# Routed experts: input sums and one pair sum on VectorE, second weight matrix issued by ScalarE

## The chip, the cores and the metric

The kernel runs on one core of a Trainium2 chip (trn2). The metric is the device time of one execution in microseconds (us). One core has a matmul engine (TensorE, PE in the profile), three engines for elementwise work (VectorE or DVE, ScalarE or ACT, GpSimd or POOL) and SyncE (SP), which issues DMAs here. Each engine works through its own queue in order, and an instruction that waits holds all that stands behind it in that queue.

## The reference

Three layers follow one another on 4608 tokens of width 512, all float32: attention in chunks of 64 tokens, a dense two-matrix layer with a squared ReLU, and a routed layer in which each token goes to the one of 8 experts with the largest logit.

```python
attn = softmax(scale * q_c @ k_c^T); x = attn @ v_c      # 8 heads, 9 chunks of 64, 8 batches
h = np.maximum(x @ w_in, 0.0); x = h * h @ w_out          # 512 -> 2048 -> 512
logits = x @ w_gate + modality_bias[modality_id]
e_idx = np.argmax(logits, axis=1)
for e in range(E):                                        # E = 8, F = 1024
    h = np.maximum(x[mask] @ w1[e], 0.0)
    out[mask] = gate_w[mask, None] * (h @ w2[e])
```

With these inputs two experts get all the tokens, 2325 and 2283. In blocks of 256 tokens that makes 10 and 9 blocks, 19 in all.

## The kernel before

Every float32 value that a matmul reads is held as two float16 words, a high word (the rounded value, made on ScalarE) and a low word (the rest, a subtraction on VectorE or GpSimd). A product is then three matmuls of word pairs. The kernel runs in two stages: attention and the dense layer on 36 tiles of 128 tokens, and then the routed layer on pairs, blocks of 256 tokens that share an expert. The tokens of a pair are gathered from DRAM by GpSimd DMAs (`x_gather`), transposed by SyncE DMAs (`x_tr`), and their outputs scattered by GpSimd DMAs (`put`), two of each for one pair.

The routed layer multiplies 2x2 block matrices with seven block products in place of eight, so a pair has seven products of the first matrix (`pair_mm1`, n = 0 to 6) and seven of the second (`pair_mm2`), and sums around them:

- `x_sum0` makes two 128x512 sums of high and low words of the input (lines 968, 969) and four 128x256 sums and differences (lines 971 to 974). `x_sum1` splits these into high words on ScalarE and low words on GpSimd (line 983).
- `pair_c` takes a product of the first matrix out of PSUM as soon as it is there and builds the four hidden blocks c11, c12, c21, c22.
- `pair_s` makes the sums of hidden blocks that the second matrix needs and splits them, in seven steps. Step 1 has the pair sum c21 = c11 - c21 on GpSimd (line 1073). Steps 5 and 6 split c12 and c21 with the low word on GpSimd (`split_h`, line 1065).
- `pair_o` takes the output products out of PSUM, scaled by the token's gate, on ScalarE (tile ms) and VectorE (tile raw), and calls `put`.

The order is written out by hand. A slot is one product with what is emitted beside it. After the first seven slots a slot of the second matrix of pair p (`run2`) alternates with a slot of the first matrix of pair p + 2 (`run1`). `plan_side(p)` is called in the slot s in which pair p's seventh product of the first matrix is emitted, and puts steps of `pair_s`, `x_sum0`, `x_sum1` and the gathers into slots s + k:

```python
if p > 2:
    once(x_tr, p + 2)
    later(3, x_gather, p + 3)
if p > 1:
    later(8 if p > 2 else 10, x_sum0, p + 2)
    later(11 if p > 2 else 13, x_sum1, p + 2)
```

The seven steps of `pair_s` have k = 1 to 7 there for pairs 2 to 17, and k = 1, 1, 2, 2, 3, 3, 4 for pair 18. For p in the middle, output products of pair p - 1 (fourth to seventh) stand at odd k up to 7, those of pair p from k = 9 on, and first-matrix products of pair p + 1 at even k. The seventh output product of pair p - 1 goes into the PSUM bank that the second one of pair p takes over, at s + 11; the two operations that empty it are on VectorE in `pair_o`. The third output product goes to the bank that the profile calls xq. The first half of a pair's output is put after its fifth product and the second half after its seventh; a put waits for the put before it to have landed.

The main part has 19 pairs (0 to 18, NP = 18). Further pairs stand in `tail`, under a condition that these inputs don't meet. `later` lets gathers and input steps through only up to pair 18; `once(x_tr, p + 2)` is not limited that way, so the transposes of pairs 19 and 20 are issued too.

The weights of a pair's expert stand in two large SBUF tiles (big0 for the first matrix, big1 for the second), which hold the dense layer's weights before. They were split earlier and wait in DRAM (wsp). Loading one matrix takes four DMAs of 0.5, 1, 1 and 1 MB (`load_part`, line 902; blocks 0, 1 to 2, 3 to 4, 5 to 6 of the seven). `early_w` loads the first expert's, all on SyncE: the first matrix before the dense layer ends; of the second matrix part 0 in the second slot of pair 1, part 1 behind the last dense tile's transposes and ahead of pair 2's, parts 2 and 3 in the sixth and seventh slot of pair 1. `late_w` issues the loads of later pairs under a condition, met where the expert changes. `x2_evac`, `x2_tr` and `route_a` to `route_c` are the evacuation, transposes and routing of a dense tile; the last tile's result is needed by the map of the later pairs (`map_b1` to `map_b3`, whose transposes on TensorE write the tile tp).

Of the kernel before, what the change touches and what calls it, by code (L numbers as in the profile page):

```python
# [31 lines left out]
def kernel(  # L32
# [13 lines left out]
    nc = tc.nc  # L46
# [850 lines left out]
        spread_pairs(ti, fs, EARLY, LATE)  # L897

    WB = [bigs[x][:, 0:14336].rearrange("p (b l k n) -> p b l k n", b=7, l=2, k=2 + 2 * x) for x in range(2)]
    def load_part(x, e, k, **kw):  # L900
        a, b = (2048 * n for n in GROUPS[k])
        nc.sync.dma_start(out=bigs[x][:, a:b], in_=wsp[bass.ds(e, 1), x, :, a:b].rearrange("a p c -> (a p) c"), **kw)

    def early_w(x, k):
        assert stored[0] >= 7 * READY * (x + 1), (x, k, stored)
        if k == 0:
            mp["ew"] = nc.sync.value_load(mp["rga"][0:1, 0:1], min_val=0, max_val=E - 1)
        load_part(x, mp["ew"], k)

    def late_w(x, p, n):  # L910
        if p >= PAIRS or n not in [b - 1 for _, b in GROUPS] or (x, p, n) in gone:
# [41 lines left out]
        x_sum1(p)  # L953

    def x_sum0(p):
        eng = nc.gpsimd
        _, t, sh, sl = xbuf(p)
        if p < 2:
            f = [a2_p.tile([128, 512], F32, tag="ee", name="xf") for _ in range(2)]
            s = [a2_p.tile([128, 2, 256], F32, tag="pt", name="xs32") for _ in range(2)]  # L960
            sv = [s[j // 2][:, j % 2] for j in range(4)]
        else:
            o = 12288
            f = [bigs[2][:, o + h * 1024:o + h * 1024 + 1024].bitcast(F32) for h in range(2)]
            s = [bigs[2][:, o + 2048 + h * 1024:o + 3072 + h * 1024].bitcast(F32).rearrange("p (j c) -> p j c", j=2) for h in range(2)]
            sv = [s[j // 2][:, j % 2] for j in range(4)]
        for h in range(2):
            (eng if p < 2 else nc.vector).tensor_tensor(out=f[h].rearrange("p (k n) -> p k n", k=4), in0=t[:, h, 0:4],
                                                        in1=t[:, h, 4:8], op=ALU.add)
        q = [[f[h][:, j * 256:j * 256 + 256] for j in range(2)] for h in range(2)]  # L970
        eng.tensor_tensor(out=sv[0], in0=q[1][0], in1=q[1][1], op=ALU.add)  # L971
        eng.tensor_tensor(out=sv[1], in0=sv[0], in1=q[0][0], op=ALU.subtract)  # L972
        eng.tensor_tensor(out=sv[2], in0=q[0][0], in1=q[1][0], op=ALU.subtract)
        eng.tensor_tensor(out=sv[3], in0=q[0][1], in1=sv[1], op=ALU.subtract)  # L974
        mp["xs", p] = s
# [91 lines left out]
    def pair_s(p, n):  # L1067
        c11, c12, c21, c22 = cbuf(p)
        if n == 0:
            split_h(p, 5, c22, AF.Relu)  # L1070
        elif n == 1:
            stt(c22, c22, 0.0, c21, ALU.max, ALU.add)
            nc.gpsimd.tensor_tensor(out=c21, in0=c11, in1=c21, op=ALU.subtract)
        elif n == 2:
            split_h(p, 1, c22)
        elif n == 3:
            nc.vector.tensor_tensor(out=c11, in0=c11, in1=c22, op=ALU.subtract)
            stt(c12, c12, 0.0, c11, ALU.max, ALU.add)
        elif n == 4:
            split_h(p, 3, c11, scale=-1.0)  # L1080
        elif n == 5:
            split_h(p, 4, c12, eng=nc.gpsimd)
        else:
            split_h(p, 6, c21, eng=nc.gpsimd)

    def pair_mm2(p, n):
        blk_, bank, first = PRODUCTS[n]
# [270 lines left out]
    for su, (b0, nt, sb) in enumerate(supers):  # L1358
# [8 lines left out]
        for t, qq in M2 if su == 0 else [(t, qq) for t in range(nt) for qq in range(4)]:  # L1367
# [17 lines left out]
            if i == NTILE - 1:  # L1385
                ch += [(T + 16.0, map_b1, ()), (T + 18.0, map_b1b, ()), (T + 21.0, map_b2, ()), (T + 22.0, meta_gather, (LATE, "b")), (T + 29.0, meta_turn, (LATE, "b")), (T + 31.0, map_b3, ())]
                ch += [(T + 34.0 + p, once, (x_gather, 4 + p)) for p in range(2)]
                ch[2:2] = [(T + d[0] + 0.1, early_w, (1, 1))]
            at_chain(ch)
        if su == len(supers) - 1:  # L1390
            at_time(TM1 + 8.0, map_a1c)
            at_time(TM1 - 8.0, rest, "a", [quad(b)[:, 0:512] for b in range(4)])
            for k in range(4):
                at_time(TM1 + 0.1 + 2.65 * k, early_w, 0, k)
            at_time(T + 0.1, early_w, 1, 0)
            for n in range(7):
                at_time(T - STEP + 1.33 * n, pair_s, 0, n)
    TEND = T
# [14 lines left out]
    with tc.manual_schedule():  # L1413
# [50 lines left out]
        def later(k, fn, *a):  # L1464
            if fn not in (x_gather, x_tr, x_sum0, x_sum1):
                side.setdefault(len(slots) + k, []).append((fn, a))
            elif a[0] <= NP:
                side.setdefault(len(slots) + k, []).append((once, (fn, *a)))

        def plan_side(p):  # L1470
            for n, k in enumerate((1, 1, 2, 2, 3, 3, 4) if p == NP else (1, 2, 3, 4, 5, 6, 7) if p > 1 else (1, 3, 4, 6, 8, 9, 10)):
                later(k, pair_s, p, n)
            if p > 2:
                once(x_tr, p + 2)
                later(3, x_gather, p + 3)
            if p > 1:
                later(8 if p > 2 else 10, x_sum0, p + 2)
                later(11 if p > 2 else 13, x_sum1, p + 2)

        slots = []  # L1480
# [4 lines left out]
        for k, fn, q in ((4, x_tr, 2), (6, x_tr, 3), (8, x_sum0, 2), (10, x_sum1, 2), (14, x_sum0, 3), (17, x_sum1, 3), (27, x_tr, 4)):  # L1485
            later(k, fn, q)
        for n in range(7):
            if n > 4:
                early_w(1, n - 3)
            run1(1, n)  # L1490
        for k in range(7 * (NP + 1)):
            run2(k // 7, k % 7)
# [85 lines left out]
```

## Time and profile before

| | |
|---|---|
| three runs | 1266.19, 1273.77, 1274.33 us, median 1273.77 |
| profiled execution | 1271.61 us, its span 1269.9 us |
| mean granted TensorE clock | 0.982 |
| TensorE matmuls | 1196.7 us busy, 94% |
| VectorE | 837.7 us, 66% |
| ScalarE | 709.3 us, 56% |
| GpSimd | 678.3 us, 53% |
| DMA | 166.26 MB, mean 131 GB/s |

The span is the time from the first to the last instruction. Busy times are those of instructions in progress, and engines overlap. A row of the timeline has the start in the span, the duration (for merged instructions that of the group, with xN), the engine, the line of the kernel, the operation, and the tiles that it writes and reads with their shape. What stands in brackets is the engine's idle time just before, and what ended it. SPq rows are DMA issues of SyncE, which are not counted as busy.

### The profile page before, as it was taken

Reading aid. Unit: us, or ns where it says so; the run is one execution under the profiler, and the core shown is the slowest. Engines: PE = TensorE matmul, PEld = TensorE weight load, DVE = VectorE, ACT = ScalarE, POOL = GpSimd, SP = SyncE. Lnnn points to the kernel's source line nnn. Section 1 sums busy time; section 2 is a strip of 40 time slices with the busy share of each in tenths; the row PEclk is TensorE's granted clock in tenths of the full one; section 3 lists DMA queues with packets and bytes.
Section 4 is the critical chain, followed back from the end, with each engine's and each line's share of the span. In section 5 each row is a group of like instructions: output and inputs, shape, how many; then the busy total and the mean of one; then the engine's idle time right before and its main releaser. Section 6 shows DMA issues by size and latency. Waiting matters only on the chain. (4 is left out here: it accounts for less than half of the span.)

```text
span 1269.9 us, 30528 instructions
## 1 busy us (share of the span) xinstructions
PE 1196.7 (94%) x12046; PEld 746.0 (59%) x12046; DVE 837.7 (66%) x1750; ACT 709.3 (56%) x1284; POOL 678.3 (53%) x626
## 2 busy tenths in 40 slices
PE   5898999999999999999999999999799998999993
PEld 4444444444445444445444444457699997889992
DVE  6899665685775765776856654625676776667751
ACT  6887673673763853854854744524355554555551
POOL 4487353471571652634651653653677766667642
PEclk9899999999999999999999999999899999999997
DMA  9456426656447356465555333257343356633431
GB/s 374 159 171 162 112 34 183 162 155 167 141 133 194 85 142 174 125 182 129 131 151 149 101 87 96 79 156 138 100 109 76 85 119 185 156 73 84 79 61 36
DMA packets 167701, 166.26 MB, mean 131 GB/s; under 512 B 124218, under 2 KB 124254, under 8 KB 166002
## 3 DMA queue, kind: packets, MB, share of 16 engines
q1 hardware_dynamic: 160226, 144.64, 42.9%
q0 software_dynamic: 7312, 19.50, 5.0%
q8 instruction: 96, 1.57, 0.6%
q14 instruction: 67, 0.55, 0.2%
HBM read 211.40 MB, written 49.16 MB: 205 GB/s over the span
## 5 line engine op out<-in xcount | busy, mean ns | idle before, releaser
L627 PE MATMUL hp<-xtall,big 128*128 128x512 f16 x1728 | 386.6, 381 | 2.6 <-ACT r L92 2.6
L642 PE MATMUL op<-big,big 128*128 128x512 f16 x1728 | 386.4, 381 | 0.5 <-POOL big L607 0.5
L642 PEld LDWEIGHTS <-big 128*128 128x128 f16 x1728 | 165.3, 98 | 194.6 <-issue 4.4
L607 POOL TENSOR_TENSOR big<-g,big 128x512 f16<-128x512 f32 x144 | 175.4, 1223 | 193.1 <-DVE g L95 92.1
L627 PEld LDWEIGHTS <-big 128*128 128x128 f16 x1728 | 164.2, 98 | 192.9 <-issue 6.4
L1024 PEld LDWEIGHTS <-big 128*128 128x128 f16 x3192 | 191.0, 99 | 6.6 <-issue 2.5
L1024 PE MATMUL hq<-big,big 128*128 128x128 f16 x2040 | 129.0, 220 | 0.7 <-DVE raw L1054 0.7
L288 POOL TENSOR_TENSOR raw<-raw 128x512 f32<-128x512 f32 x64 | 92.4, 1468 | 57.0 <-DVE ms L95 32.2
L92 ACT ACTIVATE r<-hp 128x512 f32<-128x512 f32 x138 | 81.4, 590 | 61.4 <-PE hp L627 43.9
L92 ACT ACTIVATE big<-r,bls 128x512 f16<-128x512 f32 x138 | 98.4, 714 | 3.0 <-DVE bls L101 0.6
L1092 PEld LDWEIGHTS <-xtall 128*128 128x128 f16 x840 | 80.4, 99 | 24.6 <-issue 10.8
L1092 PE MATMUL oq<-big,xtall 128*128 128x256 f16 x600 | 74.9, 276 | 14.4 <-DMA big<-wsp 7.1
L95 DVE SCALAR_TENSOR_TENSOR g<-r,bq 128x512 f32<-128x512 f32 x74 | 72.3, 979 | 20.3 <-ACT r L92 18.2
L1092 PEld LDWEIGHTS <-ho 128*128 128x128 f16 x756 | 71.9, 98 | 16.6 <-issue 9.2
L487 POOL TENSOR_TENSOR ps<-ee,ps 128x512 f16<-128x512 f32 x32 | 41.6, 1301 | 69.7 <-ACT ps L92 55.4
L712 POOL DMA_INDIRECT meta<-mt,di x36 | 39.1, 1086 | 72.2 <-issue 35.0
L1092 PE MATMUL oq<-big,ho 128*128 128x256 f16 x540 | 66.2, 273 | 8.2 <-DVE raw L95 6.0
L92 ACT ACTIVATE xs<-op 128x512 bf16<-128x512 f32 x36 | 21.4, 593 | 91.8 <-PE op L642 84.3
L92 ACT ACTIVATE xtall<-cq 128x512 f16<-128x512 f32 x70 | 43.8, 626 | 43.0 <-DVE cq L1048 14.5
L92 ACT ACTIVATE g<-r,bls 128x512 f32<-128x512 f32 x64 | 46.2, 722 | 27.4 <-POOL big L607 22.7
L92 ACT ACTIVATE big<-big 128x512 f16<-128x512 f32 (+1 forms) x58 | 37.1, 649 | 43.7 <-POOL big L972 23.1
L92 ACT ACTIVATE ho<-raw 128x512 f16<-128x512 f32 x63 | 39.4, 625 | 39.5 <-DVE raw L1048 15.6
(293 smaller groups left out, 1897.2 us busy)
## 6 DMA issues: line engine op xcount, KB each, us to landing
big<-wsp SPq DMA_DIRECT2D x114, 1024.0 KB
big<-wsp SPq DMA_DIRECT2D x38, 512.0 KB
wsp<-ms SPq DMA_DIRECT2D x75, 256.0 KB
qk<-in_qk_dram SPq DMA_DIRECT2D x36, 512.0 KB
raw<-in_w_dram SPq DMA_DIRECT2D x32, 512.0 KB
wsp<-wss SPq DMA_DIRECT2D x37, 256.0 KB
vv<-in_v_dram SPq DMA_DIRECT2D x36, 256.0 KB
x2d<-xs SPq DMA_DIRECT2D x36, 256.0 KB
```

What stands on the lines that cost most here:

```text
L92: nc.scalar.activation(out=out, in_=in_, func=func, **kw)
L95: nc.vector.scalar_tensor_tensor(out=out, in0=in0, scalar=s, in1=in1, op0=op0, op1=op1, **kw)
L288: nc.gpsimd.tensor_tensor(out=o, in0=i0, in1=i1, op=op)
L487: nc.gpsimd.tensor_tensor(out=a["ps"][:, 1], in0=pf, in1=a["ps"][:, 0], op=ALU.subtract)
L607: nc.gpsimd.tensor_tensor(out=lo, in0=q32.rearrange("p (f n) -> p f n", f=nf), in1=hi, op=ALU.subtract)
L627: nc.tensor.matmul(hp[:, q_ * n:(q_ + 1) * n], lhsT=wi[:, la, kk, f * 128:f * 128 + 128], rhs=x[:, lb, kk, :], start=i == 0, stop=i == 3 * ...
L642: nc.tensor.matmul(ps, lhsT=g[:, la, f, t * 128:t * 128 + 128], rhs=wo[:, lb, f, :], start=f == 0 and n == 0, stop=f == KF - 1 and n == 2)
L712: nc.gpsimd.indirect_dma_start(out=meta[:, :], out_offset=bass.IndirectOffsetOnAxis(ap=di[:, 0:1].bitcast(U32), axis=0), in_=mt, in_offset ...
L1024: nc.tensor.matmul(ps[:, f * 128:f * 128 + 128], lhsT=WB[0][:, n, la, kk, f * 128:f * 128 + 128], rhs=xa(lb, kk), start=first and f + m + ...
L1092: nc.tensor.matmul(ps, lhsT=hb[:, la, f * 128:f * 128 + 128], rhs=WB[1][:, n, lb, f, :], start=first and f + m == 0, stop=True, skip_group ...
```

## The change

- In `x_sum0` the four 128x256 sums of pairs 2 and later go from GpSimd to VectorE, where their two 128x512 sums are already; for pairs 0 and 1 all six stay on GpSimd.
- In `pair_s` the pair sum of step 1 goes from GpSimd to VectorE.
- Steps 5 and 6 of `pair_s` keep their low word on GpSimd, except in the last pair (18), where it goes to VectorE. For pairs 2 to 17 they move from slots s + 6 and s + 7 to s + 13 and s + 14.
- `x_sum0` moves from slot s + 8 to s + 9 for pairs above 4.
- The first expert's second matrix is issued by ScalarE in place of SyncE, with its own register load of the expert's number. Parts 0 and 1 stand ahead of the last dense tile's evacuation, parts 2 and 3 behind it.
- The gathers of pairs 19 and 20 are let through in the main part.

```diff
--- before.py
+++ after.py
@@ -897,15 +897,16 @@
         spread_pairs(ti, fs, EARLY, LATE)
 
     WB = [bigs[x][:, 0:14336].rearrange("p (b l k n) -> p b l k n", b=7, l=2, k=2 + 2 * x) for x in range(2)]
-    def load_part(x, e, k, **kw):
+    def load_part(x, e, k, eng=None, **kw):
         a, b = (2048 * n for n in GROUPS[k])
-        nc.sync.dma_start(out=bigs[x][:, a:b], in_=wsp[bass.ds(e, 1), x, :, a:b].rearrange("a p c -> (a p) c"), **kw)
+        (eng or nc.sync).dma_start(out=bigs[x][:, a:b], in_=wsp[bass.ds(e, 1), x, :, a:b].rearrange("a p c -> (a p) c"), **kw)
 
     def early_w(x, k):
         assert stored[0] >= 7 * READY * (x + 1), (x, k, stored)
+        eng = (nc.sync, nc.scalar)[x]
         if k == 0:
-            mp["ew"] = nc.sync.value_load(mp["rga"][0:1, 0:1], min_val=0, max_val=E - 1)
-        load_part(x, mp["ew"], k)
+            mp["ew", x] = eng.value_load(mp["rga"][0:1, 0:1], min_val=0, max_val=E - 1)
+        load_part(x, mp["ew", x], k, eng)
 
     def late_w(x, p, n):
         if p >= PAIRS or n not in [b - 1 for _, b in GROUPS] or (x, p, n) in gone:
@@ -953,7 +954,7 @@
         x_sum1(p)
 
     def x_sum0(p):
-        eng = nc.gpsimd
+        eng = nc.gpsimd if p < 2 else nc.vector
         _, t, sh, sl = xbuf(p)
         if p < 2:
             f = [a2_p.tile([128, 512], F32, tag="ee", name="xf") for _ in range(2)]
@@ -965,7 +966,7 @@
             s = [bigs[2][:, o + 2048 + h * 1024:o + 3072 + h * 1024].bitcast(F32).rearrange("p (j c) -> p j c", j=2) for h in range(2)]
             sv = [s[j // 2][:, j % 2] for j in range(4)]
         for h in range(2):
-            (eng if p < 2 else nc.vector).tensor_tensor(out=f[h].rearrange("p (k n) -> p k n", k=4), in0=t[:, h, 0:4],
+            eng.tensor_tensor(out=f[h].rearrange("p (k n) -> p k n", k=4), in0=t[:, h, 0:4],
                                                         in1=t[:, h, 4:8], op=ALU.add)
         q = [[f[h][:, j * 256:j * 256 + 256] for j in range(2)] for h in range(2)]
         eng.tensor_tensor(out=sv[0], in0=q[1][0], in1=q[1][1], op=ALU.add)
@@ -1070,7 +1071,7 @@
             split_h(p, 5, c22, AF.Relu)
         elif n == 1:
             stt(c22, c22, 0.0, c21, ALU.max, ALU.add)
-            nc.gpsimd.tensor_tensor(out=c21, in0=c11, in1=c21, op=ALU.subtract)
+            nc.vector.tensor_tensor(out=c21, in0=c11, in1=c21, op=ALU.subtract)
         elif n == 2:
             split_h(p, 1, c22)
         elif n == 3:
@@ -1079,9 +1080,9 @@
         elif n == 4:
             split_h(p, 3, c11, scale=-1.0)
         elif n == 5:
-            split_h(p, 4, c12, eng=nc.gpsimd)
+            split_h(p, 4, c12, eng=nc.vector if p == NP else nc.gpsimd)
         else:
-            split_h(p, 6, c21, eng=nc.gpsimd)
+            split_h(p, 6, c21, eng=nc.vector if p == NP else nc.gpsimd)
 
     def pair_mm2(p, n):
         blk_, bank, first = PRODUCTS[n]
@@ -1385,14 +1386,14 @@
             if i == NTILE - 1:
                 ch += [(T + 16.0, map_b1, ()), (T + 18.0, map_b1b, ()), (T + 21.0, map_b2, ()), (T + 22.0, meta_gather, (LATE, "b")), (T + 29.0, meta_turn, (LATE, "b")), (T + 31.0, map_b3, ())]
                 ch += [(T + 34.0 + p, once, (x_gather, 4 + p)) for p in range(2)]
-                ch[2:2] = [(T + d[0] + 0.1, early_w, (1, 1))]
+                ch[1:1] = [(T + 0.1 * k, early_w, (1, k)) for k in range(2, 4)]
+                ch[0:0] = [(T, early_w, (1, k)) for k in range(2)]
             at_chain(ch)
         if su == len(supers) - 1:
             at_time(TM1 + 8.0, map_a1c)
             at_time(TM1 - 8.0, rest, "a", [quad(b)[:, 0:512] for b in range(4)])
             for k in range(4):
                 at_time(TM1 + 0.1 + 2.65 * k, early_w, 0, k)
-            at_time(T + 0.1, early_w, 1, 0)
             for n in range(7):
                 at_time(T - STEP + 1.33 * n, pair_s, 0, n)
     TEND = T
@@ -1464,17 +1465,17 @@
         def later(k, fn, *a):
             if fn not in (x_gather, x_tr, x_sum0, x_sum1):
                 side.setdefault(len(slots) + k, []).append((fn, a))
-            elif a[0] <= NP:
+            elif a[0] <= NP or fn is x_gather and a[0] <= NP + 2:
                 side.setdefault(len(slots) + k, []).append((once, (fn, *a)))
 
         def plan_side(p):
-            for n, k in enumerate((1, 1, 2, 2, 3, 3, 4) if p == NP else (1, 2, 3, 4, 5, 6, 7) if p > 1 else (1, 3, 4, 6, 8, 9, 10)):
+            for n, k in enumerate((1, 1, 2, 2, 3, 3, 4) if p == NP else (1, 2, 3, 4, 5, 13, 14) if p > 1 else (1, 3, 4, 6, 8, 9, 10)):
                 later(k, pair_s, p, n)
             if p > 2:
                 once(x_tr, p + 2)
                 later(3, x_gather, p + 3)
             if p > 1:
-                later(8 if p > 2 else 10, x_sum0, p + 2)
+                later(9 if p > 2 else 10, x_sum0, p + 2)
                 later(11 if p > 2 else 13, x_sum1, p + 2)
 
         slots = []
@@ -1485,8 +1486,6 @@
         for k, fn, q in ((4, x_tr, 2), (6, x_tr, 3), (8, x_sum0, 2), (10, x_sum1, 2), (14, x_sum0, 3), (17, x_sum1, 3), (27, x_tr, 4)):
             later(k, fn, q)
         for n in range(7):
-            if n > 4:
-                early_w(1, n - 3)
             run1(1, n)
         for k in range(7 * (NP + 1)):
             run2(k // 7, k % 7)
```

## Rows read from the trace of the kernel before

**Rows 1.** Page of the profile, its first part, whole span.

```profile
PE 1196.7 (94%) x12046; PEld 746.0 (59%) x12046; DVE 837.7 (66%) x1750; ACT 709.3 (56%) x1284; POOL 678.3 (53%) x626
```

**Rows 2.** Timeline, TensorE: start us, duration us, engine, line, operation, out<-in.

```profile
935.61 1.47 PE L1092 MATMUL xq<-big,xtall 128*128 128x256 f16 x12
...
1032.45 1.47 PE L1092 MATMUL xq<-big,ho 128*128 128x256 f16 x12
...
1212.94 1.47 PE L1092 MATMUL xq<-big,xtall 128*128 128x256 f16 x12
...
1231.49 1.47 PE L1092 MATMUL xq<-big,ho 128*128 128x256 f16 x12
```

**Rows 3.** Waits of TensorE, 905 to 1245 us: total us, times, longest.

```profile
PE oq L1092 <- DVE raw L95: 11.6, 13, 2.1
...
PE oq L1092 <- ACT ms L92: 1.7, 2, 1.0
PE tp L759 <- DVE mgc L751: 1.2, 1, 1.2
PE hq L1024 <- DVE raw L1054: 0.7, 2, 0.3
```

**Rows 4.** Timeline of one pair, all engines; idle before in brackets.

```profile
986.77 3.06 DVE L95 SCALAR_TENSOR_TENSOR xtall<-cq,xtall 128x512 f16<-128x512 f32 x1 [0.70 <-ACT xtall L92]
986.97 2.30 POOL L1065 TENSOR_TENSOR ho<-raw,ho 128x512 f16<-128x512 f32 x2
...
989.75 0.86 DVE L95 SCALAR_TENSOR_TENSOR raw<-oq,fsb,ms 128x256 f32<-128x256 f32 x2
...
990.67 1.47 PE L1092 MATMUL oq<-big,ho 128*128 128x256 f16 x12 [0.59 <-DVE raw L95]
...
994.77 0.72 POOL L974 TENSOR_TENSOR big<-big 128x256 f32<-128x256 f32 x1
994.83 0.48 DVE L95 SCALAR_TENSOR_TENSOR raw<-xq,fsb,ms 128x256 f32<-128x256 f32 x1 [0.60 <-PE xq L1092]
...
999.02 0.69 DVE L95 SCALAR_TENSOR_TENSOR xtall<-cq,xtall 128x512 f16<-128x512 f32 x1 [0.70 <-ACT xtall L92]
...
1001.13 1.26 DVE L1065 TENSOR_TENSOR xtall<-cq,xtall 128x512 f16<-128x512 f32 x1 [0.70 <-ACT xtall L92]
```

**Rows 5.** Groups by form, 930 to 1232 us: busy us, mean ns | idle.

```profile
L95 DVE SCALAR_TENSOR_TENSOR xtall<-cq,xtall 128x512 f16<-128x512 f32 x30 | 40.1, 1336 | 16.0 <-ACT xtall L92 16.0
L95 DVE SCALAR_TENSOR_TENSOR ho<-raw,ho 128x512 f16<-128x512 f32 x32 | 38.7, 1208 | 16.9 <-ACT ho L92 16.9
...
L973 POOL TENSOR_TENSOR big<-big 128x256 f32<-128x256 f32 x15 | 15.4, 1024 | 0.0
```

**Rows 6.** Timeline, GpSimd's put where the expert changes.

```profile
1053.67 1.02 POOL L1118 DMA_INDIRECT out_dram<-raw,tib  x1 [5.44 <-DMA out_dram<-raw,tib]
```

**Rows 7.** Timeline of SyncE's DMA issues (L902 loads, L949 transposes).

```profile
819.35 2.14 SPq L902 DMA_DIRECT2D big<-wsp  x4
...
879.82 1.39 SPq L902 DMA_DIRECT2D big<-wsp  x1
881.32 5.15 SPq L949 DMA_TRANSPOSE big<-big  x2
```

**Rows 8.** Timeline, TensorE and VectorE, 886 to 901 us.

```profile
886.64 1.47 PE L1092 MATMUL oq<-big,xtall 128*128 128x256 f16 x12 [2.18 <-DMA big<-wsp]
...
892.17 0.69 DVE L968 TENSOR_TENSOR big<-big 128x512 f32<-128x512 f16 x1 [2.95 <-DMA big<-big]
...
894.38 2.74 PE L1092 MATMUL oq<-big,xtall 128*128 128x256 f16 x12 [4.93 <-DMA big<-wsp]
...
900.99 1.50 PE L1024 MATMUL hq<-big,big 128*128 128x128 f16 x24
```

**Rows 9.** Windows: busy us by engine, granted clock, DMA share, GB/s.

```profile
896.00:898.00 2.00, 2.00 (x17) 1.69 (x15) 0.57 (x1) 1.51 (x3) 2.00 (x3) 0.50 1.29 213
```

**Rows 10.** One source line, SyncE's register load: ns min/median/max.

```profile
L907 SPq TENSOR_LOAD <-rga x2: 281/282/282, 814.2 to 874.9; - x2
```

## Prediction

> **What bounds the kernel now.** I read the page first: TensorE is busy 94% of the span [rows 1], so the change can win only where TensorE waits. All its edits act behind the dense layer's last product, on the routed experts: 19 pairs of 256 tokens. Next I took a product that comes once per pair, the third of the output matrix (bank xq), and followed its starts in the timeline, from 935.61 for pair 2 to 1231.49 for pair 17: 15 periods, 295.9 us, 19.7 on average [rows 2]. The last period, 1212.94 to 1231.49, is 18.55, and in it TensorE waits for nothing, so a slot (there are 14 in a pair) is 1.325. Against that the pairs give up 295.9 - 15 x 18.55 = 17.6, the most that the steady edits can bring. The waits table says who takes it: 13 times TensorE waits for VectorE's output sums, 11.6 in all; smaller are the waits for ScalarE's scaled copies and a bank [rows 3].
>
> The timeline of one pair shows the cause [rows 4]. VectorE reads the last output bank of pair p-1 at 989.75, and the product at 990.67, which needs that bank, has waited 0.59. The operation ahead on VectorE, a low word with both inputs in SBUF, takes 3.06 where the same operation at 999.02 takes 0.69: it starts 0.2 before GpSimd's two low words (2.30 together, 1.15 each) and ends 0.56 after them. GpSimd's pair sum likewise stretches VectorE's low word at 1001.13 to 1.26. But the output operation at 994.83, with one input in PSUM, takes 0.48 beside a GpSimd sum at 994.77. So in this trace a VectorE operation with two SBUF inputs and a GpSimd one don't run at once. By groups those low words average 1336 and 1208 ns [rows 5]: (1.336 - 0.69) x 30 + (1.208 - 0.69) x 32 = 36 us of stretch, 2.4 per pair.
>
> **The pairs, edit by edit.** Times are from the end of the pair's seventh product of the first matrix, 2.65 after its neighbour xq starts; slot s+k starts at 1.325 (k-1) if TensorE never waits.
>
> Onto VectorE come the pair sum, 0.69 like its own operations of that size, and four 128x256 sums. No row has such a sum on VectorE with both inputs in SBUF. Half of 0.69 is 0.35, the 256-wide operation at 994.83 took 0.48; I take 0.45, nearer to the row that exists: 1.8. Together 2.5 more per pair. Off GpSimd go the pair sum (some 1.2, as its low words) and four sums of 0.72 to 1.02 [rows 4, 5]: 4.5.
>
> The two low words of slots s+6 and s+7 move to s+13 and s+14. Walking the new order by these durations (0.70 for VectorE's wait on a high word of ScalarE, as at 986.77): c21 and c22, the pair sum and the low words, now unstretched, keep VectorE to 7.5. The low word that took 3.06 runs 9.4 to 10.1, the output sums (0.86 for the two) to 11.0. Their reader on TensorE, slot s+11, starts at 13.25: 2.2 to spare. The input sums run 11.0 to 14.1, then c12 and its low word to 16.1; GpSimd's four low words follow one another, 16.1 to 20.7. Meanwhile VectorE has only operations that read PSUM; the first with two SBUF inputs, in the next pair, is due at 20.65. The moved low words are ready at 19.5 and 20.7, and their readers (slots s+17, s+21) start at 21.2 and 26.5. So every wait is covered, the tightest by 1.7, and the period should be TensorE's 18.55. If that cover went, each late microsecond would be paid once a pair.
>
> Where the expert changes, it does go. GpSimd's second put is held 5.44 there, until 1053.67, by the DMA of the first [rows 6], and what is queued behind it is late. Today those are the input sums, for which ScalarE waits and after it TensorE: 1.7 + 0.7 in all [rows 3]. Then the sums are free of that queue, but the moved low words lie behind it: put to 1054.7, two low words of the inputs to 1057.0, the moved one to 1058.1. That pair's zero is 1032.45 + 2.65 = 1035.1 [rows 2], its reader is due at 1056.3: 1.8 late, and the second change, near 1095, costs 1.0 by the same walk. Steady gain 17.6 - 2.8 = **14.8**; between 9 (half the waits reappears) and 17.6.
>
> The gathers for pairs 19 and 20 put four more DMAs in GpSimd's queue, ahead of two puts, as in every pair before, and SyncE's transposes of those pairs, issued today already, then wait for them. With 19 pairs nothing reads them and only conditional loads stand behind them on SyncE. Zero; if it pushes GpSimd's low words late, two waits like today's, 1.2.
>
> **The start of the pairs.** SyncE's queue puts the second matrix among waits: part two leaves at 879.82, then pair 2's transposes hold the queue 5.15 [rows 7], and parts three and four leave after them. TensorE waits 2.18 for part two, until 886.64, and 4.93 for part three, until 894.38 [rows 8]. The three products from 894.38 to 900.99 take 6.6 instead of 4.0, with the granted clock at 0.50, the lower of the two levels [rows 9]: 2.6 more.
>
> On ScalarE no row shows such an issue. SyncE's register load took 0.28 [rows 10], the four parts of the first matrix 2.14 together with little in flight, one crowded part 1.39 [rows 7]: 2.4 to 5.8 for all. I take 2.4, since the transposes are not yet in flight. Half lies ahead of the last tile's evacuation, whose transposes and routing move back by 1.2. The other half lies ahead of the second copy of a first-matrix bank, which TensorE's fifth product of pair 1 needs: about 1 of waiting there. SyncE's transposes of pair 2 move past two load parts and start about when they do now.
>
> What is late next? Pair 2's transposes: VectorE's addition waits for them until 892.17 [rows 8]. From it to the product that reads the sums, now at 900.99: addition 0.69, two sums 0.9, high word 0.70, low word 1.15, so 895.6. TensorE, without the two holes, could be there at 886.64 - 2.18 + 5 x 1.325 = 891.1, and so waits 4.5 in its turn; the slow products come back at their 2.6. Won: 900.99 - 895.6 - 2.6 = 2.8. The 1.2 that it waits for the late map (PE tp) [rows 3], whose gather stands behind GpSimd's sums, mostly goes, with one wait of pair 1 (0.6, by the usual size): 1.5. Together **4.3**. At best the transposes, alone in their queue, land 5 earlier: 9. At worst they share the engines with two parts (2 MB) that now leave ahead of them: 2 x 2.5 later, nothing won and 1 to 3 lost.
>
> **The end.** The last pair's two low words, 0.69 each on VectorE, stand ahead of output sums, against 0.57 of stretch that the pair sum no longer causes: 0, within 1.
>
> **Sum.** 1271.6 (the profiled execution) - 14.8 - 4.3 = 1252.5, **1253**. The median of the three runs is 2.2 above the profiled one; I keep the profiled scale.
>
> **Rivals.** (a) The transposes starve behind the second matrix. For: they held their issuer 5.15 with one part in flight. Against: parts one and two leave earlier and are gone by then. 14.8 won, 3 lost: **1260**. The Trainium skill says (DMA: Bandwidth & Descriptors, "Issuing engines are not separate DMA queues") that DMAs issued by different engines run on the same 16 DMA engines and interleave, and that a second issuer saves issue time only. No run shows two such queues yet. By that rule the load parts would take their time from the transposes, as in this case. 0.18.
>
> (b) The stretch moves instead of going: GpSimd's four low words, 4.6 in a row, drift into the next pair's VectorE operations. From 2.2 of delay on TensorE waits; from 2.2 + 19.7 - 18.55 = 3.4 on it is worse than today. All 4.6 gives a period of 20.95: 15 x 1.2 = 18 lost, 4.3 won, **1286**. For: VectorE has 2.5 more work per pair. Against: the walk. 0.05. The Trainium skill (SBUF — State Buffer, "Who interferes with whom") has whichever starts first hold the shared port for the whole instruction; by that rule too each GpSimd low word would take its full length.
>
> (c) GpSimd and VectorE drift in part, the period is 19.1: 9 won there, 1 at the start: **1262**. 0.12.
>
> (d) The moved sums still wait where they stand, for ScalarE, and the 2.5 of added work eats the stretch saved: the old period, 4.3 at most won: **1269**. For: 2.5 against 2.4. Against: it is the place of the stretch that costs, just ahead of the output sums. 0.03.
>
> **How the numbers follow.** Forecast 0.62, (a) 0.18, (c) 0.12, (b) 0.05, (d) 0.03. The forecast's own bounds are 17.6 + 9 won, 1245, and 9 + 3, 1260; (a) and (c) with the same play reach 1264. Range 1243 to 1264, the low end with 2 for the products' clock. One per cent, 12.7, is about what a measurement of this kernel tells from no change. Faster means 1261 or less: the forecast, most of (a), some of (c), 0.82; within: the rest of these and (d), 0.13; slower: (b), 0.05.
>
> **What would show it.** The xq starts 18.55 apart; VectorE's low words at 0.7; GpSimd's low words after the output sums; no wait for the second matrix near 886 and 894, but one of 3 to 5 for pair 2's sums. A low word stretched just after c22, a wait at the reader of the moved low words in every pair, or a ScalarE held by its four DMA issues would make it wrong.

## The result and the profile after

The changed kernel takes 1257.43 us (median of 4 runs, 1256.81 to 1260.05) against 1274.05 for the kernel before in the same job (4 runs, 1266.19 to 1276.02): ratio 0.9881, 95% interval 0.9846 to 0.9916. The profiled execution is the one of 1256.81 us; its span is 1255.1, against 1269.9 before, so 14.8 less.

Where the 14.8 lie shows if TensorE's timeline is cut at four marks: a product of the first pairs (s_all<-xgt, ahead of all that the change touches), xq of pair 2, of pair 17 and of pair 18, and the end of the span. The first mark of before:

```profile
865.18 1.50 PE L1024 MATMUL s_all<-xgt,big 128*128 128x128 f16 x24
```

And the marks of the changed kernel (the lines of [rows 2] moved on by one line in its source):

```profile
865.57 1.50 PE L1025 MATMUL s_all<-xgt,big 128*128 128x128 f16 x24
...
947.50 1.47 PE L1093 MATMUL xq<-big,xtall 128*128 128x256 f16 x12
966.05 1.47 PE L1093 MATMUL xq<-big,ho 128*128 128x256 f16 x12
...
1225.75 1.47 PE L1093 MATMUL xq<-big,ho 128*128 128x256 f16 x12
1239.30 1.47 PE L1093 MATMUL xq<-big,xtall 128*128 128x256 f16 x12
```

| stretch | before | after | difference |
|---|---|---|---|
| to the mark | 865.2 | 865.6 | +0.4 |
| start: mark to xq of pair 2 | 70.4 | 81.9 | +11.5 |
| pairs: 15 periods | 295.9 | 278.3 | -17.6 |
| last pair | 12.9 | 13.6 | +0.6 |
| end: xq of pair 18 to the end | 25.5 | 15.8 | -9.7 |

So a gain in the pairs and one behind the last product, and ahead of both a loss at the start.

**The pairs.** 947.50 to 1225.75 is 15 times 18.55, with no residue where the expert changes. Before, the periods were uneven: most of them were 18.9 to 19.8 long, two where the expert changes were 22.48 (below) and 23.50. These two give 8.9 of the 17.6, the others 8.7.

```profile
1052.28 1.47 PE L1092 MATMUL xq<-big,xtall 128*128 128x256 f16 x12
...
1074.76 1.47 PE L1092 MATMUL xq<-big,ho 128*128 128x256 f16 x12
```

TensorE's waits from 905 to 1245 us, which answer to [rows 3], were 13 for the output sums and are 3:

```profile
PE oq L1093 <- DVE raw L95: 5.3, 3, 2.6
PE cp L730 <- DVE run L95: 2.4, 1, 2.4
PE s_all L1025 <- ACT ms L92: 1.3, 2, 0.7
```

VectorE's low words, 1336 and 1208 ns in [rows 5], are no longer stretched, and its 256-wide sums (L972 to L975) take 0.42 (groups by form, 930 to 1232 us: busy us, mean ns):

```profile
L95 DVE SCALAR_TENSOR_TENSOR xtall<-cq,xtall 128x512 f16<-128x512 f32 x33 | 22.8, 692 | 17.2 <-ACT xtall L92 17.2
...
L972 DVE TENSOR_TENSOR big<-big 128x256 f32<-128x256 f32 x15 | 6.4, 426 | 1.6
```

**The start.** ScalarE issues the first three parts in 0.97 (two) and 0.34 us. Ahead of the fourth it stands until an earlier load has landed. The timeline, with SyncE's transposes of pair 2, 5.15 in [rows 7]:

```profile
876.31 0.34 ACTq L902 DMA_DIRECT2D big<-wsp  x1
...
880.14 11.14 SPq L950 DMA_TRANSPOSE big<-big  x2
...
882.74 0.34 ACTq L902 DMA_DIRECT2D big<-wsp  x1
...
883.12 0.60 ACT L92 ACTIVATE big<-hq 128x512 f32<-128x512 f32 x1 [5.28 <-DMA big<-wsp]
...
883.77 0.37 PE L1025 MATMUL hq<-xsh,big 128*128 128x128 f16 x2 [4.56 <-ACT big L92]
...
901.49 0.69 DVE L969 TENSOR_TENSOR big<-big 128x512 f32<-128x512 f16 x1 [8.57 <-DMA big<-big]
...
901.51 2.72 PE L1025 MATMUL hq<-big,big 128*128 128x128 f16 x24 [6.81 <-DMA big<-big]
```

TensorE waits 4.56 for a bank copy that stood behind ScalarE's fourth issue, and 6.81 for the transposes. The two waits for the second matrix, 7.1 together [rows 8], are gone, but with some smaller new ones TensorE's waits in this stretch come to 18.8 us against 10.0, and its products to 63.1 against 60.4, at a mean granted clock of 0.92 against 0.95: the 11.5. While the transposes stood, the DMA share was high and little was moved (windows, from the mark to xq of pair 2 before and after, and two of 4 us after; the columns as in [rows 9], at the end the granted clock, the DMA share and GB/s):

```profile
865.18:935.61 70.43, 60.40 (x771) 53.59 (x770) 42.70 (x126) 29.38 (x58) 41.37 (x39) 0.95 0.59 131
...
865.57:947.50 81.93, 63.13 (x771) 55.53 (x770) 49.22 (x141) 28.47 (x57) 28.48 (x26) 0.92 0.61 113
...
884.00:888.00 4.00, 4.00 (x54) 4.00 (x52) 2.43 (x6) 2.87 (x6) 1.28 (x2) 0.69 1.56 177
892.00:896.00 4.00, 2.71 (x27) 2.29 (x25) 0.89 (x3) 0.76 (x3) 0.00 (x0) 1.00 1.40 87
```

**The end.** GpSimd's drain at the end of the program (one source line: ns min/median/max) shrank from 9.37 us, in the profile before,

```profile
L1573 POOLq DRAIN  x3: 46/107/9372, 1259.7 to 1269.6; - x3
```

to 0.88 in the profile after:

```profile
L1572 POOLq DRAIN  x3: 46/107/878, 1253.4 to 1254.8; - x3
```

### The profile page after: what moved, and what is told of

Same layout as the page of the kernel before. It is cut to its first block, busy times and chain, and to the rows that moved or that the text cites. A ratio compares the mean times of both kernels' runs of the same rounds, so it can differ in the third digit from the quotient of the medians.

```text
span 1255.1 us, 30508 instructions
## 1 busy us (share of the span) xinstructions
PE 1195.6 (95%) x12046; PEld 746.2 (59%) x12046; DVE 833.3 (66%) x1839; ACT 707.4 (56%) x1284; POOL 601.8 (48%) x541
## 5 line engine op out<-in xcount | busy, mean ns | idle before, releaser
L1119 POOL DMA_INDIRECT out_dram<-raw,tib x30 | 35.3, 1178 | 90.3 <-DVE raw L95 75.0
L984 POOL TENSOR_TENSOR big<-big 128x512 f16<-128x512 f32 x34 | 39.5, 1179 | 60.0 <-ACT big L92 60.0
L92 ACT ACTIVATE big<-hq 128x512 f32<-128x512 f32 x56 | 33.4, 596 | 61.2 <-PE hq L1025 54.1
```

What stands on the lines that cost most here:

```text
L92: nc.scalar.activation(out=out, in_=in_, func=func, **kw)
L984: eng.tensor_tensor(out=sl[:, 2 * h:2 * h + 2], in0=s[h], in1=sh[:, 2 * h:2 * h + 2], op=ALU.subtract)
L1119: nc.gpsimd.indirect_dma_start(out=out[:, :], out_offset=bass.IndirectOffsetOnAxis(ap=t.bitcast(U32), axis=0), in_=o, in_offset=None, boun ...
```

## The experiments

Twelve kernels, in three jobs. The kernel before took 1274.35 (first job), 1272.03 (second) and 1273.11 us (third). Four stretches from the profile of each, cut at the same marks. The stretch ahead of the first mark, which no edit touches, ends between 863.2 and 868.6 in these profiles, so two or three microseconds between two totals can come from there:

| kernel | median us | ratio, 95% interval | start | pairs | last pair | end |
|---|---|---|---|---|---|---|
| before | 1274.05 | | 70.4 | 295.9 | 12.9 | 25.5 |
| after | 1257.43 | 0.9881 (0.9846, 0.9916) | 81.9 | 278.3 | 13.6 | 15.8 |
| e1_sync_loads | 1248.16 | 0.9796 (0.978, 0.9812) | 72.4 | 278.3 | 13.6 | 15.6 |
| e2_scalar_loads_only | 1279.74 | 1.0049 (1.0016, 1.0083) | 86.2 | 294.2 | 12.9 | 25.5 |
| e3_slots_only | 1271.81 | 0.9989 (0.9966, 1.0012) | 70.7 | 292.8 | 12.9 | 25.8 |
| e4_sums_only | 1257.68 | 0.986 (0.9837, 0.9884) | 72.1 | 278.3 | 12.4 | 25.4 |
| e5_early_one_queue | 1245.72 | 0.9798 (0.9771, 0.9824) | 71.5 | 278.3 | 13.6 | 15.7 |
| e6_three_parts | 1244.54 | 0.9786 (0.9761, 0.981) | 70.0 | 278.3 | 13.5 | 16.3 |
| e7_no_gathers | 1263.12 | 0.9917 (0.9888, 0.9946) | 78.0 | 278.2 | 13.6 | 25.1 |
| e8_gathers_only | 1265.12 | 0.9935 (0.991, 0.9959) | 69.9 | 299.7 | 12.9 | 18.3 |
| e9_fourth_later | 1246.23 | 0.9795 (0.9773, 0.9817) | 70.1 | 278.3 | 13.6 | 16.6 |
| e10_old_slots | 1245.89 | 0.98 (0.9774, 0.9826) | 68.4 | 278.3 | 12.4 | 19.0 |
| e11_input_sums | 1259.88 | 0.9907 (0.9879, 0.9936) | 71.2 | 284.4 | 12.9 | 25.9 |
| e12_pair_sum | 1254.88 | 0.9855 (0.9827, 0.9882) | 70.7 | 278.3 | 12.4 | 25.8 |

The first four take the change apart.

**e1_sync_loads**: the changed kernel with the second matrix back on SyncE, at its old places.

```diff
-        eng = (nc.sync, nc.scalar)[x]
+        eng = nc.sync
```

> The changed kernel with one part undone: the second weight matrix is issued by SyncE again, at its old places. Theory Q: the start of the pairs lost 11.9 us (the xq product of pair 2 starts at 947.5 instead of 935.6) because loads from ScalarE's queue and pair 2's transposes from SyncE's queue were in flight together. Then this run wins that back: xq of pair 2 near 936, periods still 18.55, about 1246 us. Rival V: the start lost because the input sums on VectorE stand ahead of the map of the later pairs. Then xq of pair 2 stays near 947 and the time at 1257.

The start is back at 72.4, and 9.3 us of the median come back. The loads are what costs there.

**e2_scalar_loads_only**: the kernel before, with only the second matrix's issues moved to ScalarE, at the change's early places.

```diff
+        eng = (nc.sync, nc.scalar)[x]
...
-        load_part(x, mp["ew"], k)
+        load_part(x, mp["ew", x], k, eng)
...
-                ch[2:2] = [(T + d[0] + 0.1, early_w, (1, 1))]
+                ch[1:1] = [(T + 0.1 * k, early_w, (1, k)) for k in range(2, 4)]
+                ch[0:0] = [(T, early_w, (1, k)) for k in range(2)]
...
-            if n > 4:
-                early_w(1, n - 3)
```

> The kernel before with only the second weight matrix moved to ScalarE. Theory Q: the two holes for the weights go, but TensorE waits some 11 us for ScalarE and for pair 2's transposes: xq of pair 2 near 947, periods as before (19.7 on average), about 1285 us. Rival V: the holes go and nothing else comes, xq of pair 2 near 931, about 1269.

Slower than before, by 0.2 to 0.8%. Its ten runs spread from 1271.92 to 1289.13, and the profiled one (1285.77) lies 6 above their median; so the 15.7 lost at its start is probably more than the usual loss. The same pair of events stands in its timeline, the transposes longer still:

```profile
879.90 15.92 SPq L950 DMA_TRANSPOSE big<-big  x2
...
882.07 0.60 ACT L92 ACTIVATE big<-hq 128x512 f32<-128x512 f32 x1 [4.63 <-DMA big<-wsp]
```

**e3_slots_only**: the kernel before, with only the two low words in later slots.

```diff
-            for n, k in enumerate((1, 1, 2, 2, 3, 3, 4) if p == NP else (1, 2, 3, 4, 5, 6, 7) if p > 1 else (1, 3, 4, 6, 8, 9, 10)):
+            for n, k in enumerate((1, 1, 2, 2, 3, 3, 4) if p == NP else (1, 2, 3, 4, 5, 13, 14) if p > 1 else (1, 3, 4, 6, 8, 9, 10)):
```

> The kernel before with only the two GpSimd low words moved from slots 6 and 7 to 13 and 14 (and no other edit). Theory P: what costs is where GpSimd's low words stretch VectorE, just ahead of the output sums. Then the period of the xq product falls to 18.55 to 18.8 and the time by 14 to 17, to some 1258. Rival W: VectorE and ScalarE must also be freed of GpSimd's input sums and pair sum. Then the period stays at 19.2 or more and the time above 1268.

No difference that can be measured. The low word that took 3.06 takes 0.69 here too (988.95 in its timeline), so the stretch ahead of the output sums is gone, and the time is not: 3.1 are won in the pairs. With its old sums still in GpSimd's queue, the moved words come too late for their readers (TensorE's waits, 905 to 1245 us):

```profile
PE oq L1092 <- POOL xtall L1065: 4.1, 6, 0.9
PE oq L1092 <- POOL ho L1065: 3.3, 5, 0.9
PE oq L1092 <- DVE raw L95: 2.5, 2, 2.0
```

**e4_sums_only**: the kernel before, with the four input sums and the pair sum on VectorE, and no slot moved.

```diff
-        eng = nc.gpsimd
+        eng = nc.gpsimd if p < 2 else nc.vector
...
-            nc.gpsimd.tensor_tensor(out=c21, in0=c11, in1=c21, op=ALU.subtract)
+            nc.vector.tensor_tensor(out=c21, in0=c11, in1=c21, op=ALU.subtract)
```

> The kernel before with only the four input sums and the pair sum moved from GpSimd to VectorE; the low words stay in slots 6 and 7. Theory P: the stretch ahead of the output sums stays (3.06 us for the low word), and VectorE has 2.4 us more per pair: period 19.3 to 20, time 1268 to 1280. Rival W: less GpSimd work is what helps, period 18.55 to 18.8 and about 1258.

The full 17.6 in the pairs, without moving a low word. So the sums bring it, and the question became which.

**e11_input_sums** and **e12_pair_sum**: one line of e4's diff each.

> The kernel before, with the four 128x256 input sums on VectorE alone; the pair sum stays on GpSimd. The two together brought the period from 19.7 to 18.55 us. If GpSimd's 3.3 us of input sums, for which ScalarE and then TensorE waited, are what mattered, this one has 18.55 or nearly, and takes 1257 to 1260 us. If it is the pair sum, which stands ahead of the low words on GpSimd and on VectorE stretches one of its own, this one stays at 19.5 to 19.7 and 1270 to 1276 us.

> The kernel before, with the pair sum of step 1 on VectorE alone; the input sums stay on GpSimd. If the input sums are what mattered, the period stays at 19.5 to 19.7 us and the time at 1270 to 1276. If the pair sum is, 18.55 to 18.8 and 1257 to 1261. If each gives a part: about 19.1 in both and 1264 to 1267.

Neither "the one or the other" nor "a part each": the pair sum alone does all of it, the input sums alone two thirds. The pair sum gives 18.55 a period, the whole 17.6. The input sums give 18.87 in nearly every period and 11.5 in all; 8.2 of these come from the two periods in which the expert changes. In e12 GpSimd's first low word runs before VectorE's and the second behind it:

```profile
1003.19 1.15 POOL L1065 TENSOR_TENSOR xtall<-cq,xtall 128x512 f16<-128x512 f32 x1 [0.95 <-ACT xtall L92]
...
1004.83 0.69 DVE L95 SCALAR_TENSOR_TENSOR ho<-raw,ho 128x512 f16<-128x512 f32 x1 [0.70 <-ACT ho L92]
...
1005.40 1.16 POOL L1065 TENSOR_TENSOR xtall<-cq,xtall 128x512 f16<-128x512 f32 x1 [1.07 <-ACT xtall L92]
```

In e11 the stretch of [rows 4] stands where it stood, and the product behind it waits 0.16 in place of 0.59:

```profile
1004.36 0.68 DVE L1042 TENSOR_TENSOR raw<-s_all,big 128x512 f32<-128x512 f32 x1
...
1005.74 3.07 DVE L95 SCALAR_TENSOR_TENSOR ho<-raw,ho 128x512 f16<-128x512 f32 x1 [0.69 <-ACT ho L92]
1005.95 2.29 POOL L1065 TENSOR_TENSOR xtall<-cq,xtall 128x512 f16<-128x512 f32 x2
...
1009.65 1.47 PE L1092 MATMUL oq<-big,xtall 128*128 128x256 f16 x12 [0.16 <-DVE raw L95]
```

**e7_no_gathers** and **e8_gathers_only** take the gathers of pairs 19 and 20 from the changed kernel, and give them alone to the kernel before (e8's edit; e7's is the reverse).

```diff
-            elif a[0] <= NP:
+            elif a[0] <= NP or fn is x_gather and a[0] <= NP + 2:
```

> The changed kernel without the gathers for pairs 19 and 20. In the kernels with them GpSimd's drain at the end of the program takes 0.88 us, in those without 9.37. If the gathers decide that, this one drains 9.37 us and takes 1266 to 1268 us. If the drain goes by something else (less work on GpSimd, ScalarE's or VectorE's share), it stays at 0.88 us and the time at 1256 to 1259 us.

> The kernel before, with the gathers for pairs 19 and 20 alone. If these decide the drain at the end: 0.88 us there and, with the other waits as before, 1263 to 1266 us in all. If they don't: 9.37 us and 1273 to 1276 us, more if the four gathers hold GpSimd's sums up in the last pairs.

The drain goes with the gathers, 9.37 without and 0.88 with them. In e7:

```profile
L1572 POOLq DRAIN  x3: 46/107/9372, 1253.3 to 1263.2; - x3
```

In e8:

```profile
L1573 POOLq DRAIN  x3: 46/107/878, 1264.7 to 1266.2; - x3
```

e8 is faster than before by 0.4 to 0.9%. Its last two periods are 19.32, where those of before are 18.55, which is 1.5 of the 3.8 by which its pairs are longer: there the kernel before has no gathers left in GpSimd's queue. e7's median, 1263.1, lies below the 1266 to 1268 expected. Its profiled run took 1265.3; its start cost 78.0 and not 81.9, but its first mark came 3.0 later.

The next three, and e9, are about the start.

**e5_early_one_queue**: the changed kernel's early places, all on SyncE (e1's line alone).

> The changed kernel, with the second matrix's four parts issued at the same early places in the program, but by SyncE. Two theories of the 11.5 us that the changed kernel loses up to pair 2 (first-matrix product of the last pair of dense tiles at 865 us to pair 2's xq: 70.4 us before, 81.9 after, 72.4 with the loads back at their old places). Two queues: what costs is that ScalarE's parts run beside SyncE's transposes, each taking turns. One queue in this order then gives pair 2's xq at 72 to 76 us behind that mark and 1246 to 1251 us in all. Order: what costs is that parts 2 and 3 (2 MB) go ahead of pair 2's transposes at all, on whichever queue. Then 80 to 84 us behind the mark, and 1255 to 1259 us.

**e6_three_parts**: the last part on SyncE, in the sixth slot of pair 1, behind the issue of pair 2's transposes.

```diff
+        if (x, k) == (1, 3):
+            mp["ew", 2] = nc.sync.value_load(mp["rga"][0:1, 0:1], min_val=0, max_val=E - 1)
+            load_part(1, mp["ew", 2], 3)
+            return
...
-                ch[1:1] = [(T + 0.1 * k, early_w, (1, k)) for k in range(2, 4)]
+                ch[1:1] = [(T + 0.1 * k, early_w, (1, k)) for k in range(2, 3)]
...
         for n in range(7):
+            if n == 5:
+                early_w(1, 3)
             run1(1, n)
```

> The changed kernel, with the last part of the second matrix (1 MB) issued by SyncE behind pair 2's transposes, the other three by ScalarE as in the change. In the changed kernel ScalarE stood 5.28 us at the fourth part until an earlier load had landed. If this hold of ScalarE is the cost, the 11.5 us shrink by about 5, to 1252 us, and the transposes of pair 2 take their 11 us still. If the two queues side by side are the cost, three quarters of it stay for 2.5 of 3.5 MB: 1254 to 1256 us, with the transposes at 8 to 10 us. If all of it comes from the fourth part, the start is that of the kernel before: 1246 to 1248 us.

**e9_fourth_later**: as e6, but the last part stays on ScalarE; only its place moves.

```diff
-                ch[1:1] = [(T + 0.1 * k, early_w, (1, k)) for k in range(2, 4)]
+                ch[1:1] = [(T + 0.1 * k, early_w, (1, k)) for k in range(2, 3)]
...
         for n in range(7):
+            if n == 5:
+                early_w(1, 3)
             run1(1, n)
```

> The changed kernel, with the second matrix's last part (1 MB) issued in the sixth slot of pair 1 by ScalarE; the first three parts stay at their early places on ScalarE. With that last part on SyncE at this place the start was that of the kernel before (first-matrix product at 863 us to pair 2's xq: 70.0 us; 81.9 in the changed kernel) and the time 1244.5 us. If what the changed kernel loses is ScalarE standing at its fourth issue until an earlier load has landed, ScalarE no longer stands here, the start takes 70 to 73 us and the whole 1244 to 1248. If it is the fourth megabyte on a second queue beside the transposes of pair 2, these take 9 to 11 us again, the start 77 to 82, and the whole 1251 to 1257.

All three start like the kernel before: 71.5, 70.0, 70.1. The early places in the program are not the cost (e5), three parts on a second queue are not (e6), nor the fourth on that queue (e9). What is left is the fourth issue on ScalarE at its early place, where it can't go out yet. In e9 it comes some 3 us later, when the issue of pair 2's transposes is nearly done; ScalarE doesn't stand, and the transposes take 5.76:

```profile
880.57 5.76 SPq L950 DMA_TRANSPOSE big<-big  x2
...
885.90 0.34 ACTq L902 DMA_DIRECT2D big<-wsp  x1
...
892.21 0.69 DVE L969 TENSOR_TENSOR big<-big 128x512 f32<-128x512 f16 x1 [0.90 <-DMA big<-big]
```

What was to be won at the start is not won either. The waits of 2.18 and 4.93 for the second matrix are gone in e9, and others have come in their place, for the last dense tile's routing above all, whose steps stand in VectorE's queue behind the sums that were moved there (TensorE's waits, 866 to 936 us):

```profile
PE cp L730 <- DVE run L95: 3.5, 1, 3.5
PE oq L1093 <- DVE raw L95: 2.6, 1, 2.6
PE lp L670 <- DMA x2t<-xs: 1.4, 1, 1.4
```

The expectation had this kernel as the test of ScalarE's hold against a megabyte beside the transposes. It doesn't part them: both vanish together, as both came together in the changed kernel, in e2 and in e7.

**e10_old_slots**: e6 with the low words back in slots s + 6 and s + 7 (for pair 18 on GpSimd), the input sums at s + 8.

> The kernel with three parts of the second matrix on ScalarE and the last on SyncE (1244.5 us), with the low words of c12 and c21 back in slots s+6 and s+7, the input sums back at s+8, and the last pair's low words on GpSimd. If sums on VectorE alone give the full period, as in the run with the sums alone, the pairs stay 18.55 apart, the last xq comes 12.4 rather than 13.55 behind the one before, and the whole takes 1243 to 1245 us. If the place of the low words is needed once the start is quicker, the period goes to 19 or more and the time to 1251 or more.

The same time as e6, as far as the two intervals tell. The last pair is 1.1 quicker. The end is 2.7 longer: GpSimd's two low words (2.29 us) are again among its last puts, and these leave 4.1, 9.6 and 13.6 behind the last xq, against 2.9, 6.4 and 10.4 in the changed kernel.

## Why the prediction was right and wrong

The direction was right, and 1253 stands 4 from the 1256.81 of the profiled run. That closeness is luck: the start came out 16 worse than forecast, the pairs 2.8 better, and the last pair and the end 9.1 better. Without these 9.1 the time would be near 1266, outside the stated range.

**The pairs: right in size, wrong in the reason.** The walk gave a period of 18.55 with every wait covered, and that is what came. The 2.8 kept back for the expert change was mis-sized; it measured 0. It rested on the put's hold of 5.44 [rows 6]. In the changed kernel the put in that place of the schedule leaves at 1054.91, 14.7 behind its pair's xq (1040.25); in [rows 6] it left 21.2 behind (1053.67 - 1032.45), and GpSimd's next work then still waits 2.65 for ScalarE, so the hold delays nothing. What the expert change costs in the kernel before was mis-sized too: the text reads 1.7 + 0.7 from [rows 3], and the two periods give 8.9.

The step that failed is "it is the place of the stretch that costs, just ahead of the output sums". In e3 the place is empty and 3.1 of 17.6 are won, though there the moved words are late for their readers; in e11 the stretch stays, and a steady period is still cut by 0.44 of the 0.76 that it is too long, while what the expert change cost is gone. What the runs showed in its place is a chain that closes on itself without TensorE. Six rows of the kernel before carry it (timeline, all engines, 985 to 1005 us):

```profile
985.39 0.68 DVE L1042 TENSOR_TENSOR cq<-s_all,big 128x512 f32<-128x512 f32 x1
...
990.54 1.28 DVE L968 TENSOR_TENSOR big<-big 128x512 f32<-128x512 f16 x2
...
995.52 0.63 ACT L92 ACTIVATE big<-big 128x512 f16<-128x512 f32 x1 [1.18 <-POOL big L974]
...
996.42 0.58 ACT L92 ACTIVATE big<-s_all 128x512 f32<-128x512 f32 x1
...
997.03 0.69 DVE L1053 TENSOR_TENSOR cq<-hq,big 128x512 f32<-128x512 f32 x1 [1.72 <-ACT big L92]
...
1004.70 0.68 DVE L1042 TENSOR_TENSOR raw<-s_all,big 128x512 f32<-128x512 f32 x1
```

After L1042 come the low word of 3.06 and the output sums [rows 4], then VectorE's input sums (990.54), then GpSimd's, then ScalarE's high words, which wait for these, then a bank copy in ScalarE's queue (996.42), for which VectorE waits, then the hidden blocks up to the next L1042, 19.31 behind the first. TensorE needs 18.55 and waits for the rest.

Where the expert changes, the kernel before lengthens this ring by itself. GpSimd's put, held 5.44 [rows 6], stands ahead of its sums; ScalarE waits 4.25 for these, VectorE 4.91 for ScalarE, and the round takes 22.49 where the period is 22.48:

```profile
1044.35 0.68 DVE L1042 TENSOR_TENSOR raw<-s_all,big 128x512 f32<-128x512 f32 x1
...
1056.29 0.63 ACT L92 ACTIVATE big<-big 128x512 f16<-128x512 f32 x1 [4.25 <-POOL big L972]
...
1059.17 0.69 DVE L1053 TENSOR_TENSOR raw<-hq,big 128x512 f32<-128x512 f32 x1 [4.91 <-ACT big L92]
...
1066.84 0.68 DVE L1042 TENSOR_TENSOR cq<-s_all,big 128x512 f32<-128x512 f32 x1
```

So in a steady period a cut counts until once round is 18.55, which takes 0.76, and beyond that it only covers rounds that are held up. With the pair sum gone from GpSimd, the low word takes 0.69 in place of 3.06: enough three times over, and the period is 18.55. With the input sums gone, ScalarE waits no more for GpSimd, but the stretch stays: 18.87, a cut of 0.44; what sets the 18.87 was not followed. And in the last two periods of before, without gathers in GpSimd's queue, the low word is not stretched and the period is 18.55; e8 gives the gathers back and it is 19.32. The chain is read off the rows; that it sets the period is argued from these kernels and from the held round, and no run lengthened it on purpose.

**The low words' new slots: costless, and not needed.** They cost 0 in the changed kernel's pairs, as walked; the wait of rival (b) and the 19.1 of (c) did not come, with the 256-wide sums at 0.42 for the 0.45 taken. The rule named under (b), that whichever starts first keeps the port, is not what [rows 4] show: VectorE's low word started 0.2 before GpSimd's two and was the one stretched, to 3.06, while GpSimd's took 2.30 together. But e3 shows them worth nothing alone, and e10 nothing in the best version.

**The start: the sign was wrong.** Forecast 4.3 won; 11.5 lost. Two steps failed. The issues took 1.65, under the 2.4 taken, but ScalarE stood 5.28 ahead of the fourth, 6.9 together and past the upper bound of 5.8. The text named "a ScalarE held by its four DMA issues" as what would make it wrong, but priced it at about 1 on TensorE; it was 4.56. And pair 2's transposes, which "start about when they do now", did (880.14 against 881.32) but took 11.14 in place of 5.15. Rival (a), the transposes behind the second matrix, came, with a wait of 6.81 on TensorE where it had 3 lost in all, and ScalarE's hold beside it. Without that harm the 4.3 was not there either: e9 and the kernel before differ by 0.3. TensorE's next wait came not where the text saw it, at the product that reads pair 2's sums, but at the last tile's routing behind these sums in VectorE's queue (3.5) and at output sums (2.6).

What the Trainium skill says of this (DMA: Bandwidth & Descriptors, "Issuing engines are not separate DMA queues"), that DMAs of several issuers interleave on the same engines and a second issuer saves only issue time, agrees with the trace in its first half: from 884 to 888 us of the changed kernel two queues move data side by side, 0.53 and 0.17 MB. The second half no run here tests, since in e9 and e6 other waits took what a quicker load could have won. The rule doesn't by itself give the 11.5: in e9 three parts on ScalarE's queue leave the transposes at 5.76.

What stays open: why the transposes take 11 to 16 us when the fourth part comes out 1.5 to 2.6 us behind their first issue (e2, e7 and the changed kernel) and 5.76 when it comes 5.3 behind (e9), which of the two harms brings how much of the 11.5, and why the fourth issue waits at all. No run tried the fourth part at the early place on a queue that holds no other work.

**The end: a term that wasn't in the sum.** The gathers were put at zero, with 1.2 if they made low words late. They took 9.3 us off the end in the changed kernel (25.1 in e7, 15.8 with them), and 7.2 in e8. Only the transposes of those pairs read what they gather, and no product reads these. Why a drain should be shorter after two more gathers, no run says. The last pair's forecast, 0 within 1, measured 0.6.

**What the best version is.** e6: 1244.54 us, 1.0% below the changed kernel in terms of their ratios to before (0.9786 against 0.9881). e5, e9, e10 and e1 are the same within the intervals. By the runs that take the edits one at a time, the pair sum, the gathers, and any place of the loads at which no engine stands should be all it takes; no kernel with these alone was run.

## What to carry to other kernels

Before pricing a stall by the row beside it, follow the chain back until it meets itself: a cut in a ring of several engines pays out only down to the period that the busiest engine, here TensorE, needs for itself, so of two cuts that are each enough the second is worth nothing in a steady round, and a cut elsewhere in the ring can do what the cut at the stall does. A DMA issue handed to a compute engine should be priced by what stands behind it in that engine's queue if the issue can't go out, not by its own 0.34 us; place it where earlier loads have landed. Account for the whole span, the last 20 us too, since a term that nothing computes with can outweigh the one under study.

## What was not expected of the hardware

- GpSimd's drain at the end of a program has two lengths, 9.37 us in seven profiles without the gathers of pairs 19 and 20 (before, e2, e3, e4, e7, e11, e12) and 0.88 in seven with them.
- An issue on ScalarE takes 0.34 us, but ahead of the fourth ScalarE stood 5.28 (4.63 in e2, 4.16 in e7) until a part issued earlier had landed.
- The issue of pair 2's two transposes on SyncE took 5.15 to 5.38 us in the kernels without loads on ScalarE's queue, 5.76 to 6.98 behind three of them (e6, e9, e10), and 11.14 to 15.92 when the fourth came out among them (e2, e7 and the changed kernel); in the changed kernel the DMA engines then moved 87 GB/s at a share of 1.40, where [rows 9] has 213 at 1.29.
- Four 128x256 sums with both inputs in SBUF take 0.42 each on VectorE; on GpSimd they took 0.72 to 1.22.
